# State scaling and diagonal copies moved from VectorE to ScalarE, with loads and selections re-ordered in the first four chunks

## The chip, the cores and the metric

The kernel runs on one core of one Trainium2 chip. The metric is the device time of one execution in microseconds (us). Each engine of the core has its own queue of instructions and works through it in order: TensorE (PE for its matmuls, PEld for its weight loads), VectorE (DVE), ScalarE (ACT), GpSimd (POOL) and SyncE (SP), which here only issues transfers. An instruction that waits for a semaphore holds up everything behind it on the same engine.

## What is computed

A recurrence over time (an RWKV-like attention with a decay) for 4 sequences, 8 heads, 768 steps and head size 48; its output, as 3072 tokens of 384 features, goes through three matrices, their maximum, and a fourth matrix. In short:

```python
for t in range(768):                       # r, k, v, w: (4, 8, 768, 48)
    cur = einsum('bhd,bhe->bhde', u * k[t], v[t])
    y[:, :, t] = einsum('bhd,bhde->bhe', r[t], state + cur)
    state = w[t][..., None] * state + einsum('bhd,bhe->bhde', k[t], v[t])
x = y.transpose(0, 2, 1, 3).reshape(3072, 384)
out = maximum(maximum(x @ w1, x @ w2), x @ w3) @ w_out      # 384 -> 768 -> 384
```

The four matrices arrive in 64-bit floats, the rest in 32-bit.

## The kernel before

Time is cut into chunks of 128 steps, 6 to a sequence, 24 in all (k = 0 to 23). Four chunks make a half of 512 tokens for the second part ("MLP"), of which there are six. The first half is worked with plain 32-bit matmuls.

The order of work is written out by hand. `FRONT` is a string of steps for the first four chunks and the start of the first half; each step is a letter with a chunk number, and each engine meets its own instructions in the string's order. The letters that matter here:

- `b`, `f` the two decay scans of a chunk (L360 and L374, DVE; `b` also copies the chunk's decay to `dec`, L362, ACT); `s` the reciprocal between them; `r` scales k and r (L385, L386, DVE); `d` multiplies r by k for the diagonal (L399, DVE, needs the chunk's second load); `D` sums that on PE (L411).
- `e` copies the diagonal's sums out of PSUM to `cs` (L419), lets POOL select them into the matrix `a` (L427), and issues the load of the next chunk's v (L229, SP). The buffer of chunk 4's v is chunk 1's, so its load waits for chunk 1's last values on PE.
- `X` scores (L449, PE), `M` takes them into `a` (L458, DVE), `T` transposes k (L469, PE) with a copy to `kn` (L471, ACT), `R` reads the state (L482, PE), `U` forms the new state (L492, L496, PE), `S` scales it by the decay into `sstar` (L507), `V` and `Z` make the values (L527, PE), `E` copies them to x (L545, ACT) and, after chunks 2 and 3, issues small transfers within x (L554), three by SP and three by ACT.
- `c` squares the scans for an overflow test (L391, ACT). `n` loads a chunk (L241, SP, two parts). `w` loads one weight tile (L287, SP). `i` converts one (L303, ACT; a later step does L312 and L314 on DVE). `W` runs filler matmuls (L573). `m` and `p` run a group of the MLP, which starts on the x of three chunks (L147), adds the fourth (L155), and goes on with whole groups (L167); the maximum of a group's three results starts with a copy `h_hi` (L130, ACT), which also frees one of three PSUM banks, and goes on with L133 (DVE).

After `FRONT`, `START` and two loops run the rest in the same manner.

Of the kernel before, what the change touches and what calls it, by code (L numbers as in the profile page):

```python
# [34 lines left out]
ALU = mybir.AluOpType  # L35
AF = mybir.ActivationFunctionType
# [4 lines left out]
B, H, S, D = 4, 8, 768, 48  # L41
DM, FF = 384, 768
NP = 4
# [10 lines left out]
CPH = HT // C  # L54
# [12 lines left out]

FRONT = ("b0 s0 f0 d0 W2 D0 W3 r0 X0 T0 W3 c0 e0 b1 s1 d1 D1 U0 f1 W4 R0 e1 M0 V0 Z0 E0 S0 n3 r1 "  # L70
# [3 lines left out]
TURN = "b1 d1 w | f1 w | D1 r1 c1 | e1 M0 w | "  # L74
ORD = "w R0 V0 U0 X1 Z0 E0 b2 d2 | f2 n3 w | D2 S0 r2 c2 | e2 M1 w | T1 w | |"

# [18 lines left out]
def kernel(ctx: ExitStack, tc, tin, nat, u_flat, u_pair, v_t, w_all, out, ytr):  # L95
    nc = tc.nc
# [99 lines left out]
    with ExitStack() as fast:  # L196
# [23 lines left out]
        def load_nat(k):  # L220
            b, c = divmod(k, NCH)
            if k in natt:
                return
            vt = v_p.tile([128, DM], F32, name="v")
            kr = None
            if k >= CS:
                kr = nat_p.tile([128, 2, DM], F32, name="kr")
                nc.sync.dma_start(out=kr[:, :, :], in_=nat[b, c, :, 1:3, :])
            nc.sync.dma_start(out=vt[:, :], in_=nat[b, c, :, 0, :])  # L229
            natt[k] = (vt, kr)  # L230
# [39 lines left out]
        sstar = [cst.tile([128, NP, 64], F32, name=f"sstar{i}") for i in range(2)]  # L270
        dec = [cst.tile([128, LINE], F32, name=f"dec{i}")[:, 0:NP] for i in range(2)]
# [83 lines left out]
        prep = {k: {} for k in range(NK)}  # L355
# [59 lines left out]
        def prep_diag2(k):  # L415
            ahead("D", k)
            cs = small.tile([128, LINE], F32, name="cs")[:, 0:H]
            if k < CS:
                nc.vector.tensor_copy(out=cs[:, :], in_=prep[k]["ps"][:, 0:H])  # L419
            else:  # L420
                nc.vector.tensor_reduce(out=cs[:, :].rearrange("p (a b) -> p b a", a=2),  # L421
                                        in_=natt[k][1][:, 0, :].rearrange("p (b a d) -> p b a d", a=2, d=D),
                                        axis=AX.X, op=ALU.add)
            a = a_p.tile([128, 4, 3, HC], F32, name="a")
            for lo in (0, HC):
                rows = slice(lo, lo + HC)
                nc.gpsimd.affine_select(out=a[rows, :, 0:2, :], pattern=[[0, 4], [0, 2], [1, HC]],  # L427
                                        in_=cs[rows, :].rearrange("p (a b) -> p a b", b=2).unsqueeze(3).broadcast_to([HC, 4, 2, HC]),
                                        compare_op=ALU.is_equal, fill=0.0, base=0, channel_multiplier=-1)
            prep[k]["a"] = a  # L430
            if k + 1 < NK:
                load_nat(k + 1)
# [28 lines left out]
        def goes_on(k):  # L461
            return k % NCH < NCH - 1
# [36 lines left out]
        def state(k):  # L499

            if goes_on(k):
                new = prep[k]["pu"][0:112, 0:NP * D].rearrange("p (a b) -> p a b", a=NP)
                if k % NCH > 0 and k >= CPH:
                    cur = scur[0:112, :].rearrange("p (a b) -> p a b", a=NP)
                    nc.vector.tensor_tensor(out=cur, in0=new, in1=sstar[k % 2][0:112, :, 0:D], op=ALU.add)
                    new = cur
                nc.vector.tensor_tensor(out=sstar[(k + 1) % 2][0:112, :, 0:D], in0=new,  # L507
                                        in1=dec[(k + 1) % 2][0:112, :].unsqueeze(2).broadcast_to([112, NP, D]), op=ALU.mult)

        def after(later, sooner):  # L510

# [27 lines left out]
        def result(k):  # L539
# [11 lines left out]
            for lo in (0, 64) if cols else ():  # L551
                for j in range(KT):
                    eng = nc.scalar if lo and half < PLAIN else nc.sync
                    eng.dma_start(out=x[lo + 48:lo + 64, j, cols], in_=x[lo + 16 * j:lo + 16 * j + 16, KT, cols])  # L554

        steps = dict(X=scores, M=take, T=transposes, R=from_state, U=to_state, S=state, V=values, Z=values2, E=result, n=load,
                     b=prep_scan_b, s=prep_start, f=prep_scan_f, r=prep_rk, c=prep_check, d=prep_diag1,
                     D=prep_diag_sum, e=prep_diag2)
        ready = {("n", k) for k in range(3)}

        def ahead(step, k):

            if k < NK and (step, k) not in ready:
                ready.add((step, k))
                steps[step](k)
# [107 lines left out]
        def take_x(early=False):  # L673
            h = len(xs)
            there = ("E", CPH * (h + 1) - 2) in ready if early else units >= min(UPH * (h + 1) + XD, UPC * NK)
            if h < NH and there and groups >= GPH * h - 2 * CPH:
                xs[h] = x_parts(h)
# [39 lines left out]
        simple = dict(p=part, a=unit, c=weights, i=begin, w=load_w, m=group, f=fix, x=lambda: take_x(True))  # L717
        for step in FRONT.split():
            if step in simple:
# [14 lines left out]
    with tc.If(verdict[0] != 0, label="general"), ExitStack() as slow:  # L734
        pool = lambda name, bufs, **kw: slow.enter_context(tc.tile_pool(name=name, bufs=bufs, **kw))
        c1 = pool("c1", 1)
# [7 lines left out]
        with tc.For_i(0, B) as b:  # L744
            for pr in range(NP):
# [8 lines left out]
                for hh in range(2):  # L754
                    rows = slice(64 * hh, 64 * hh + 48)
                    for t, o in ((wt, pr * WS + 1), (rt, WC + pr * C), (kt, WC + NP * C + pr * C)):
                        for c in range(NCH):
                            for lo in (0, HC):
                                at = o + (HC - lo if t is kt and pr % 2 == 0 else lo)
                                nc.sync.dma_start(out=t[rows, c * C + lo:c * C + lo + HC],  # L760
                                                  in_=tin[ds(b, 1), c, rows, at:at + HC].rearrange("a p n -> (a p) n"))
                    nc.sync.dma_start(out=uc[rows, :], in_=u_pair[pr, hh])
                nc.vector.tensor_scalar(out=uk[0:112, :], in0=kt[0:112, :], scalar1=uc[0:112, :], scalar2=None, op0=ALU.mult)
                for j in range(KT):
                    with tc.For_i(0, 16) as i:
# [5 lines left out]
                        for hh in range(2):  # L771
                            nc.sync.dma_start(
                                out=vb[64 * hh:64 * hh + 48, :],
                                in_=v_t[ds(b, 1), 2 * pr + hh, ds(i + 16 * j, 1), :].rearrange("a e t -> (a e) t").broadcast_to([48, S]))
# [22 lines left out]
        for i in range(NW if w_all.dtype != F32 else 0):  # L797
# [5 lines left out]
            low, scale = raw[:, 0:2 * PC:2], sc[:, :].bitcast(F32)  # L803
# [16 lines left out]
        with tc.For_i(0, NH) as half:  # L820
            x = xs_p.tile([128, KT, HT], F32, name="x")
# [73 lines left out]
```

## Time and profile before

| | |
|---|---|
| runs, us | 413.6, 413.74, 414.51 (median 413.74) |
| profiled execution | 413.68 us, its span 412.0 us |
| PE busy | 400.9 us, 97% of the span |
| DVE, ACT, POOL busy | 279.4, 151.3, 80.6 us |
| granted TensorE clock | 1.00 throughout |
| instructions | 9165 |

Times in rows count from the start of the span. The execution's own time is 1.7 us longer than its span. PE is busy almost without a break from 34.4 us to the end; the first 34 us, where the first four chunks run one after another, have DVE busy for 9.14 to 9.86 us of every 10 us from 10 us on.

### The profile page before, as it was taken

To read this page: it belongs to the slowest core of one execution; us is meant where nothing else is said; L and a number is where in the kernel's file an instruction comes from. 1 tells how busy PE (TensorE), PEld (TensorE's weight loads), DVE (VectorE), ACT (ScalarE), POOL (GpSimd) and SP (SyncE) were. 2 spreads that over 40 slices of the span, in tenths; PEclk is the share of its full clock that TensorE was granted. 3 is DMA by queue.
4 is the path that set the end of the run, shared out by engine and by line. 5 is a ranking of instruction groups with operands and counts; after the bars stand their busy time and mean duration, and the time that the engine had idled before them with its cause. 6 is when DMAs were issued, how large, how long until landed. Compare 5 with 4: busy or idle time off the path is not lost.

```text
span 412.0 us, 9165 instructions
## 1 busy us (share of the span) xinstructions
PE 400.9 (97%) x3729; PEld 315.6 (77%) x3729; DVE 279.4 (68%) x511; ACT 151.3 (37%) x318; POOL 80.6 (20%) x96
## 2 busy tenths in 40 slices
PE   6989999999999999999999999999999999999994
PEld 2656454556688889988889988889988888988894
DVE  6989999989869969848777658678666622233320
ACT  1344434233535532525433644433622321311211
POOL 2410032233222211213122212223123200000000
PEclk9999999999999999999999999999999999999999
DMA  8594994641550330595563686751550000300001
GB/s 210 157 324 143 335 312 140 208 139 40 152 176 23 105 111 17 139 286 163 176 184 113 158 267 212 228 154 43 180 168 2 0 2 2 97 1 0 2 15 66
DMA packets 24126, 54.09 MB, mean 131 GB/s; under 512 B 3312, under 2 KB 9776, under 8 KB 24080
## 3 DMA queue, kind: packets, MB, share of 16 engines
q1 hardware_dynamic: 20160, 43.43, 34.2%
q10 hardware_dynamic: 3920, 10.03, 8.1%
q8 instruction: 30, 0.49, 0.5%
q14 instruction: 16, 0.13, 0.1%
HBM read 47.55 MB, written 4.72 MB: 127 GB/s over the span
## 4 chain that ended last, share of the span: by engine, by line
PE 94%; DMA 1%; ACT 1%; issue 1%; SPq 1%; POOL 0%; POOLq 0%; ACTq 0%
PE psm L167 56%; PE psm L187 16%; PE gram L449 5%; PE y L527 5%; PE tu L492 3%; PE y L482 3%; PE psm L573 2%; PE tu L469 2%; DMA out_dram<-m 1%; PE psm L411 1%; PE psm L147 1%; SPq L554 1%; DMA x<-x 0%; PE psm L155 0%; PE tu L496 0%
## 5 line engine op out<-in xcount | busy, mean ns | idle before, releaser
L167 PE MATMUL psm<-x_hi,w 128*128 128x512 f32 x540 | 172.8, 394 | 0.2 <-ACT m L191 0.2
L167 PEld LDWEIGHTS psm<-x_hi,w 128*128 128x128 f32 x540 | 101.4, 188 | 22.0 <-ACT m L191 0.8
L167 PE MATMUL psm<-x_lo,w 128*128 128x512 f32 x270 | 105.3, 390 | 0.0
L133 DVE TENSOR_TENSOR m<-psm,m 128x512 f32<-128x512 f32 x60 | 41.1, 685 | 58.9 <-PE psm L167 44.5
L187 PE MATMUL psm<-w,h_hi 128*128 128x384 f32 x288 | 78.2, 364 | 0.0
L427 POOL TENSOR_SCALAR_AFFINE_SELECT a<-cs 64x512 f32<-64x512 f32 x48 | 37.1, 774 | 143.4 <-DVE cs L421 92.6
L167 PEld LDWEIGHTS psm<-x_lo,w 128*128 128x128 f32 x270 | 50.8, 188 | 9.8
L187 PEld LDWEIGHTS psm<-w,h_hi 128*128 128x128 f32 x288 | 51.8, 188 | 6.5 <-DVE w L314 0.4
L167 PE MATMUL psm<-x,w 128*128 128x512 f32 x96 | 42.6, 597 | 0.0
L545 ACT COPY x<-y 112x512 f32<-112x512 f32 x24 | 14.1, 586 | 75.2 <-PE y L527 74.7
L402 POOL TENSOR_TENSOR kr<-kr 128x384 f32<-128x384 f32 x18 | 21.1, 1172 | 99.8 <-PE y L527 88.5
L187 PE MATMUL psm<-w,h_lo 128*128 128x384 f32 x120 | 40.3, 336 | 0.0
L391 ACT ACTIVATE gf<-gf 112x1034 f32<-112x1034 f32 x24 | 25.7, 1070 | 35.6 <-DVE tin L386 35.2
L110 ACT CAST h_hi<-m 128x512 fp32r<-128x512 f32 x30 | 18.7, 622 | 53.7 <-DVE m L133 53.7
L374 DVE TENSOR_TENSOR_SCAN gf<-tin,d_fwd 112x517 f32<-112x517 f32 x24 | 36.1, 1502 | 0.7
L167 PEld LDWEIGHTS psm<-x,w 128*128 128x128 f32 x96 | 17.8, 190 | 20.4 <-issue 19.1
L360 DVE TENSOR_TENSOR_SCAN gf<-tin,d_bwd 112x517 f32<-112x517 f32 x24 | 29.9, 1246 | 4.8 <-DMA tin<-in_tin_dram 4.7
L111 DVE TENSOR_TENSOR h_lo<-m,h_hi 128x512 fp32r<-128x512 f32 x30 | 20.6, 688 | 16.7 <-ACT h_hi L110 16.7
L527 PE MATMUL y<-a,v 64*48 64x64 f32 (+3 forms) x768 | 25.7, 246 | 0.6 <-POOLq L534 0.2
L458 DVE COPY_PREDICATED a<-mask,gram 128x384 f32<-128x384 int32 x48 | 25.3, 581 | 0.5 <-PE gram L449 0.5
L527 PEld LDWEIGHTS y<-a,v 64*64 64x64 f32 (+1 forms) x768 | 21.6, 126 | 4.7 <-issue 3.1
L130 ACT COPY m<-psm 128x512 f32<-128x512 f32 x30 | 17.5, 582 | 16.4 <-PE psm L167 9.8
(72 smaller groups left out, 424.9 us busy)
## 6 DMA issues: line engine op xcount, KB each, us to landing
tin<-in_tin_dram SPq DMA_DIRECT2D x23, 448.0 KB, 5.1
w<-in_w_all_dram SPq DMA_DIRECT2D x24, 384.0 KB, 7.2
cv<-in_w_all_dram ACTq DMA_DIRECT2D x24, 384.0 KB, 3.6
kr<-in_nat_dram SPq DMA_DIRECT2D x18, 384.0 KB, 5.8
tin<-in_tin_dram SPq DMA_DIRECT2D x23, 231.0 KB, 3.5
v<-in_nat_dram SPq DMA_DIRECT2D x24, 192.0 KB, 5.5
out_dram<-m SPq DMA_DIRECT2D x24, 192.0 KB, 2.6
x<-x SPq DMA_DIRECT2D x30, 32.0 KB, 2.0
```

The source lines that it names most:

```text
L111: rest = lambda: nc.vector.tensor_tensor(out=lo, in0=src, in1=hi.bitcast(F32), op=ALU.subtract)
L133: nc.vector.tensor_tensor(out=m[:, :], in0=ps[:, :], in1=m[:, :], op=ALU.max)
L167: nc.tensor.matmul(ps[:, :], lhsT=wt[f * 3 + wi][:, ct * 128:(ct + 1) * 128], rhs=xt[:, ct, :], start=(n == 0), stop=(n == KT * len(terms) ...
L187: nc.tensor.matmul(pss[tt][:, 0:DM], lhsT=ht[f][:, tok], rhs=wt[FT * 3 + f][:, :], start=(f == 0 and i == 0), stop=(f == FT - 1 and i == l ...
L360: nc.vector.tensor_tensor_scan(out=gf[0:112, 0, ::-1], data0=t[0:112, 0:WC][:, ::-1], data1=d_bwd[0:112, ::-1], initial=0.0, op0=ALU.mult, ...
L374: nc.vector.tensor_tensor_scan(out=gf[0:112, 1, :], data0=tbuf[k % NB][0:112, 0:WC], data1=d_fwd[0:112, :], initial=0.0, op0=ALU.mult, op1 ...
L391: nc.scalar.activation(out=flat, in_=flat, func=AF.Square, accum_out=acc[0:112, k:k + 1])
L402: nc.gpsimd.tensor_tensor(out=n[:, 0, :], in0=n[:, 0, :], in1=n[:, 1, :], op=ALU.mult)
L427: nc.gpsimd.affine_select(out=a[rows, :, 0:2, :], pattern=[[0, 4], [0, 2], [1, HC]], in_=cs[rows, :].rearrange("p (a b) -> p a b", b=2).un ...
L449: nc.tensor.matmul(to, lhsT=p["kp"][q:q + 48, pr, lo:lo + HC], rhs=p["rp"][q:q + 48, pr, HC * late:C], start=(hh, lo) not in begun, stop=T ...
L458: nc.vector.copy_predicated(out=p["a"][:, 2 * hh:2 * hh + 2, :, :].rearrange("p a b c -> p a (b c)"), mask=mask_b(2), data=p["gs"][hh].rea ...
L527: mm = nc.tensor.matmul(p["y"][64 * half:64 * half + m, hh, j, HC * late:C], lhsT=natt[k][0][lo:lo + HC, h * D:h * D + m], rhs=a[:, j, :] ...
```

## The change

`e` copies the sums by ACT for chunks 0 to 5, where DVE did it. `S` scales the state of chunks 0 to 3 by four ACT instructions, one per pair of heads, where one DVE instruction did it. In `FRONT`, `e` of chunks 0, 2 and 3 stands ahead of the transposes (with it goes the load of the next chunk's v), `S` of chunks 0 to 2 stands directly behind `U` or one step later, the loads of chunks 4 and 5 and of the weights change places, and the third conversion `i` stands behind chunk 2's copy to x.

```diff
-FRONT = ("b0 s0 f0 d0 W2 D0 W3 r0 X0 T0 W3 c0 e0 b1 s1 d1 D1 U0 f1 W4 R0 e1 M0 V0 Z0 E0 S0 n3 r1 "
-         "W2 X1 d2 D2 T1 c1 b2 s2 e2 R1 U1 M1 V1 Z1 E1 f2 S1 n4 w w w r2 "
-         "W4 X2 d3 D3 T2 c2 b3 s3 e3 w w R2 U2 n5 i i i M2 V2 Z2 E2 f3 S2 r3 "
-         "W3 X3 d4 T3 R3 M3 x V3 Z3 E3 w w U3 p p w w c n6 w m D4 b4 s4 c c3 S3 m w f4 c e4 m r4 c X4 T4 R4 c4 w w")
+FRONT = ("b0 s0 f0 d0 W2 D0 W3 r0 X0 e0 T0 W3 c0 b1 s1 d1 D1 U0 f1 W4 R0 e1 S0 M0 V0 Z0 E0 n3 r1 "
+         "W2 X1 d2 D2 e2 T1 c1 b2 s2 R1 U1 S1 M1 V1 Z1 E1 f2 r2 "
+         "W4 X2 d3 D3 e3 w w w n4 w T2 c2 b3 s3 R2 U2 S2 i i M2 V2 Z2 E2 i n5 f3 r3 "
+         "W3 X3 d4 T3 R3 M3 x V3 Z3 E3 w w w U3 p p w c n6 w m D4 b4 s4 c c3 S3 m w f4 c e4 m r4 c X4 T4 R4 c4 w w")
...
-                nc.vector.tensor_copy(out=cs[:, :], in_=prep[k]["ps"][:, 0:H])
+                nc.scalar.copy(out=cs[:, :], in_=prep[k]["ps"][:, 0:H])
...
-                nc.vector.tensor_tensor(out=sstar[(k + 1) % 2][0:112, :, 0:D], in0=new,
-                                        in1=dec[(k + 1) % 2][0:112, :].unsqueeze(2).broadcast_to([112, NP, D]), op=ALU.mult)
+                for pr in range(NP) if k < CPH else ():
+                    nc.scalar.activation(out=sstar[(k + 1) % 2][0:112, pr, 0:D], in_=new[:, pr, :], func=AF.Identity,
+                                         scale=dec[(k + 1) % 2][0:112, pr:pr + 1])
+                if k >= CPH:
+                    nc.vector.tensor_tensor(out=sstar[(k + 1) % 2][0:112, :, 0:D], in0=new,
+                                            in1=dec[(k + 1) % 2][0:112, :].unsqueeze(2).broadcast_to([112, NP, D]), op=ALU.mult)
```

Lines from 508 on lie four further down in the changed kernel (L554 becomes L558). PE's instructions stand in the same order before and after.

SP's queue before, from the load of chunk 3's v on (`v` is L229; `tin_115` is chunk 4's buffer and `tin_116` chunk 5's; `w` are weight tiles):

```order
L229 DMA v<-in_nat_dram 128x384
L241 DMA tin_115<-in_tin_dram 112x528
L241 DMA tin_115<-in_tin_dram 112x1024
L287 DMA w<-in_w_all_dram 128x384 x3
L229 DMA v<-in_nat_dram 128x384
L287 DMA w<-in_w_all_dram 128x384 x2
L241 DMA tin_116<-in_tin_dram 112x528
L241 DMA tin_116<-in_tin_dram 112x1024
L554 DMA x<-x 16x384 x3
L554 DMA x<-x 16x128 x3
L287 DMA w<-in_w_all_dram 128x384 x4
```

SP's queue now, the same stretch:

```order
L229 DMA v<-in_nat_dram 128x384 x2
L287 DMA w<-in_w_all_dram 128x384 x3
L241 DMA tin_115<-in_tin_dram 112x528
L241 DMA tin_115<-in_tin_dram 112x1024
L287 DMA w<-in_w_all_dram 128x384
L558 DMA x<-x 16x384 x3
L241 DMA tin_116<-in_tin_dram 112x528
L241 DMA tin_116<-in_tin_dram 112x1024
L558 DMA x<-x 16x128 x3
L287 DMA w<-in_w_all_dram 128x384 x4
```

Chunk 4's v and three weight tiles stand ahead of chunk 4's load, four weight tiles instead of five stand ahead of the transfers within x, and the fifth tile stands behind the second set of them.

ACT's queue before, from the second set of transfers within x on (`cv` is the conversion of the next weight tile, here the fourth to the seventh):

```order
L554 DMA x<-x 16x128 x3
L303 ACTIVATE cv<-w,minus_two 128x384
L362 COPY dec_137<-gf 112x4
L303 ACTIVATE cv<-w,minus_two 128x384
L391 ACTIVATE gf,acc<-gf 112x1034
L130 COPY h_hi<-psm 128x512
L303 ACTIVATE cv<-w,minus_two 128x384 x2
```

ACT's queue now, the same stretch:

```order
L558 DMA x<-x 16x128 x3
L303 ACTIVATE cv<-w,minus_two 128x384
L362 COPY dec_137<-gf 112x4
L303 ACTIVATE cv<-w,minus_two 128x384
L391 ACTIVATE gf,acc<-gf 112x1034
L508 ACTIVATE sstar_135<-tu,dec_137 112x48 x4
L130 COPY h_hi<-psm 128x512
L303 ACTIVATE cv<-w,minus_two 128x384
L419 COPY cs<-psm 128x8
L303 ACTIVATE cv<-w,minus_two 128x384
```

The conversions of the fourth and fifth tile stand where they stood; four scalings of chunk 3's state now stand ahead of the copy `h_hi`, and the copy of chunk 4's sums stands between the sixth and seventh tile's conversions.

## Rows read from the trace of the kernel before

**Rows 1.** The page, busy time by engine, and instruction queue (packets, MB, share):

```profile
PE 400.9 (97%) x3729; PEld 315.6 (77%) x3729; DVE 279.4 (68%) x511; ACT 151.3 (37%) x318; POOL 80.6 (20%) x96
...
q8 instruction: 30, 0.49, 0.5%
```

**Rows 2.** Who waited for whom, PE, whole span (total us, times, longest):

```profile
PE tu L492 <- issue: 1.4, 1, 1.4
PE psm L167 <- ACT m L191: 0.2, 1, 0.2
```

**Rows 3.** Chain of waits, 20 to 48 us (start, us, what):

```profile
25.74 1.35 issue
...
34.53 3.87 PE psm L147 x12
...
40.49 2.58 PE psm L167 x6
```

**Rows 4.** Timeline of DVE (start, us, instruction, idle time before and its releaser):

```profile
9.35 0.17 DVE L419 COPY cs<-psm 128x8 f32<-128x8 f32 x1 [0.27 <-PE psm L411]
...
20.60 0.32 DVE L507 TENSOR_TENSOR sstar<-tu,dec 112x192 f32<-112x192 f32 x1
20.84 0.90 DVE L385 TENSOR_TENSOR tin<-tin,gf 112x256 f32<-112x256 f32 x2
...
28.00 0.36 DVE L507 TENSOR_TENSOR sstar<-tu,dec 112x192 f32<-112x192 f32 x1 [0.79 <-ACT cv L303]
...
29.54 0.75 DVE L399 TENSOR_TENSOR kr<-tin 112x256 f32<-112x256 f32 x2
30.77 1.05 DVE L458 COPY_PREDICATED a<-mask,gram 128x384 f32<-128x384 int32 x2 [0.47 <-PE gram L449]
```

**Rows 5.** Timeline of PE, up to 46 us:

```profile
21.34 1.04 PE L573 MATMUL psm<-warm 128*128 128x512 bf16 x4
...
29.73 0.90 PE L449 MATMUL gram<-tin 48*64 48x128 f32 x32
...
40.33 2.74 PE L167 MATMUL psm<-x,w 128*128 128x512 f32 x6
```

**Rows 6.** Timeline of SP's issues, 18 to 38 us:

```profile
18.80 0.79 SPq L241 DMA_DIRECT2D tin<-in_tin_dram  x2
...
21.47 0.33 SPq L229 DMA_DIRECT2D v<-in_nat_dram  x1
...
35.63 2.00 SPq L287 DMA_DIRECT2D w<-in_w_all_dram  x4
```

**Rows 7.** DMA issues at 15.99, 21.47, 35.63, then 35.63 with 36.26: us to landing

```profile
v<-in_nat_dram SPq DMA_DIRECT2D x1, 192.0 KB, 2.4
...
v<-in_nat_dram SPq DMA_DIRECT2D x1, 192.0 KB, 6.4
...
w<-in_w_all_dram SPq DMA_DIRECT2D x1, 384.0 KB, 3.4
...
w<-in_w_all_dram SPq DMA_DIRECT2D x2, 384.0 KB, 4.3
```

**Rows 8.** Busy time by stretch, 26 to 30 us (last: clock, DMA share, GB/s):

```profile
26.00:30.00 4.00, 2.79 (x47) 1.76 (x51) 3.21 (x7) 2.44 (x6) 0.13 (x1) 1.00 1.04 351
```

**Rows 9.** Timeline of ACT, 25 to 40 us:

```profile
25.97 0.19 ACT L362 COPY dec<-gf 112x4 f32<-112x4 f32 x1
26.06 1.93 ACT L303 ACTIVATE cv<-w,minus_two 128x384 f32<-128x384 uint32 x3
...
36.61 0.65 ACT L303 ACTIVATE cv<-w,minus_two 128x384 f32<-128x384 uint32 x1
37.16 1.05 ACT L391 ACTIVATE gf<-gf 112x1034 f32<-112x1034 f32 x1
38.12 0.19 ACT L391 ACTIVATION_READ_ACCUMULATOR gf<-gf 112x1 f32 x1
39.10 0.58 ACT L130 COPY h_hi<-psm 128x512 f32<-128x512 f32 x1 [0.80 <-PE psm L155]
```

## The prediction, on record before the changed kernel ran

> **What bounds the kernel now.** I read the page first: PE is busy for 97% of the span [rows 1]. So the second question is where PE waits at all, and the list of its waits has next to nothing: one gap of 1.4 us in the front, called "issue", and 0.2 us much later [rows 2]. The chain of waits says the same in order of time: from 34.5 us on it runs along PE, L147, L155 and L167 without a break [rows 3]. What follows has a fixed length as long as PE never waits. The time therefore changes by two things only: how early PE enters L147, and whether it is held up afterwards. The timelines of the front tell the rest. There DVE sets the pace, and its last long wait is the one for U of chunk 2, behind PE's gap [rows 3, 4].
>
> **What DVE is spared.** The first copy of sums takes 0.17 us, after a wait of 0.27 us for PE; without it the next scan starts about 0.4 us sooner [rows 4]. The later copies are worth some 0.06 us each, since they overlap with their neighbours. The state scaling of chunk 1 takes 0.24 us of DVE's queue (20.60 to 20.84), that of chunk 2 as much again and a wait of 0.79 us that would only grow were DVE earlier [rows 4]. By the end of chunk 1 DVE is 1.0 us ahead (0.4, two scalings of 0.25, two copies). PE is less ahead, because its values and fillers of that chunk stay: I take 0.4 us at the end of chunk 1's second values (before: 21.34, where the fillers begin [rows 5]), with 0 and 0.8 as ends. The selections ahead of the transposes cost nothing: POOL has 20% of its time in use [rows 1], and its order is unchanged. What the added copies cost ACT in chunks 0 to 3 is covered too: ACT waits for PE or DVE before most of what it does there.
>
> **PE's gap.** At 25.74 PE stops for 1.35 us [rows 3] and nothing it needs is missing. PE's 7458 instructions stand against 30 packets of 16 KB on the instruction queue [rows 1], so some 249 fit a packet, and I read the gap as a packet that came late through transfers that were queued from 18.80 on [rows 6]. In the changed order nothing large is issued between chunk 3's v (15.99) and the end of chunk 1's values, so this packet should come in time and the gap go. Then chunk 2's values end near 27.0, about 2 us sooner, and with them DVE's wait for U.
>
> **What is late next.** Chunk 4's load is. On SP it used to be issued at 18.80; now it stands behind the load of chunk 4's v, which waits for chunk 1's second values as it did before (issued 21.47, just after 21.34 [rows 5, 6]), and behind three weight tiles. So it starts after about 21.07 (21.47 less 0.4). Its landing: before, the same six loads (231 and 448 KB of chunk 4, three tiles of 384 KB, 192 KB of v, 2023 KB in all) were issued from 18.80 on, and the last landed at 21.47 + 6.4 = 27.87 [rows 6, 7], 9.07 us after the first issue. The same bytes from 21.07 on end at 30.1, and now chunk 4's second part is the last. That is the nearest row, and I take it. The other end: a lone v lands in 2.4 us [rows 7], of which its 197,000 bytes take 0.56 us at 351 GB/s [rows 8], so 1.84 us are fixed; with 2.07 MB at that rate (5.9 us) the six end 7.7 us after 21.07, at 28.8. A later end, 30.6, is had with no gain on PE and 0.1 us more.
>
> DVE's multiply of chunk 4 (L399) needs that load, and chunk 3's take (L458) stands behind it on DVE. Before, L399 started at 29.54 and could have released the take 0.65 us later, but the take waited for scores until 30.77 [rows 4]. Now L399 starts at about 30.15 and the take at 30.8. **Nothing is left of the gain**: chunk 3's values, U and L147 stand where they stood, within -2.0 (the take can't precede the scores, 29.73 before [rows 5] plus 0.9 and then about 2 us sooner) and +0.5 us. The weights for L147 are converted by DVE right behind the take and move with it. The transfers within x after chunk 2 are issued by ACT and SP around 28 to 31 instead of 29.73 on, behind two conversions instead of three, and have landed well before L147. Chunk 5's load, now behind them, is wanted only at chunk 5, 12 us later, and costs nothing.
>
> **What is added: the fifth weight tile.** It used to be issued before chunk 5's load. Now it stands on SP behind the second transfers within x, in the place that the sixth tile had: issued at 35.63, landing 3.4 us later, at 39.03 [rows 6, 7]. Its conversion stands on ACT ahead of the overflow square, of the four new scalings and of `h_hi`, and was done at 36.61 before [rows 9]. So ACT now waits until 39.06. From there by rows 9: conversion to square 0.55 (36.61 to 37.16), square to its accumulator 0.96 (37.16 to 38.12), 0.09 to the next (as 25.97 to 26.06), then four scalings. For those no row exists; the copies of decay are the nearest, small ones of 0.19 us that follow each other by 0.09 us, so four take 0.36 to 0.8 us; I take 0.5, near the lower end since they queue without waits. `h_hi` then starts at 39.06 + 0.55 + 0.96 + 0.09 + 0.5 = 41.16 and ends 0.58 later, at 41.74, where before it started at 39.10 [rows 9]. PE's next group (L167, third tile) writes the bank that `h_hi` empties; it started at 40.33 [rows 5] and now starts at 41.8: **a new wait of 1.45 us**. Queued behind `h_hi` are L133 on DVE, and behind that chunk 4's scaling of r and scores; these move by about as much and add nothing of their own. The ends: with the tile landing in 3.0 us (as the fixed 1.84 and 1.12 for its bytes) and four scalings at 0.36, 0.9; with 4.3 us, what the median of two tiles shows [rows 7], and 0.8, 2.65.
>
> [...]
>
> **Sum.** Profiled execution 413.68 us (0.06 under the median of the runs); entry into L147 unchanged (0.0), new wait +1.45: **415.1 us**.
>
> **Rivals.**
> 1. *Chunk 4's load lands early.* At 28.8 the take starts at 29.5 instead of 30.77: 413.68 - 1.3 + 1.45 = 413.8. For it: six loads at the rate of rows 8 would do so. Against: the same six took 9.07 us before. It decides at about 29.4: landing before that, the kernel is not slower by more than 0.2%. This is the other side.
> 2. *Early load and early tile.* If the take reaches the scores (-2.0) and the new wait is only 0.9 to 1.1, 412.7. For it: PE could be up to 0.8 us ahead when v is issued. Against: it needs both ends at once.
> 3. *PE's next instruction packet comes late.* The backlog now lies 2.3 us later, across the packet after the one that was late; a second gap like the first adds 1.35: 416.5. For it: rows 3 show one such gap under such a backlog. Against: nothing after it showed one, though transfers were queued. [...]
>
> **Chances.** Differences under 0.2% (0.8 us) can hardly be told from no change here. Forecast 0.55 (its own range 414.3 to 416.2, of which 0.05 lies under 414.5), rival 1 0.20, rival 2 0.12, rival 3 0.13. So slower by over 0.2% 0.50 + 0.13 = 0.63, within 0.05 + 0.20 = 0.25, faster 0.12. The range leaves out most of rival 2 and the upper half of rival 3: 412.9 to 416.5.
>
> **What would show it.** Right: no gap in PE before chunk 2's U; L399 of chunk 4 waiting for `tin` until about 30; L147 within 0.5 us of 34.5; ACT waiting for `w` until about 39; L167 of the third tile waiting for `h_hi`, starting near 41.8, and no PE wait after that. Wrong: L399 without a wait, or L147 before 33 (rival 1, 2); another gap called "issue" (rival 3); `h_hi` before 40, which would mean that the fifth tile came earlier than I read from SP's order.

## The result: 1.3% slower, and outside the range

The changed kernel takes **419.28 us** (median; 418.43 to 419.49), the kernel before 413.85 us on the same chip: ratio **1.0131, 95% interval 1.0108 to 1.0154**, 5.4 us more. The direction was forecast, the size was not: 415.1 us, with 416.5 as the upper end. The profiled execution took 418.43 us, the shortest of the four, with a span of 416.6 us (before: 413.68 and 412.0). Executions of one kernel differ with the clock: of 25 of the kernel before, the ten with a mean granted clock of 0.998 or more took 413.05 us on the mean and the three below 0.990 416.17, and the profiled one had 1.000, while all of the kernel after had 0.986 to 0.990.

In the changed file the lines from the state scaling on stand four further down: the values L527 are now L531, the fillers L573 are L577. First PE's list of waits in the kernel after (engine, line, releaser: total us, times, longest), which had two rows of note before [rows 2]:

```profile
PE y L531 <- DVE a L458: 4.1, 1, 4.1
...
PE psm L167 <- ACT h_hi L130: 1.2, 1, 1.2
```

PE's gap of 1.35 us is gone, as forecast. The wait for `h_hi` is there, 1.2 us long, as forecast (a wait of 3.2 us at the start, which is left out here, is the same in either kernel). But there is a wait of 4.1 us for chunk 3's take, which the prediction had put at nothing. The timeline of PE shows both and what lies between (start, us, instruction, idle time before it and its releaser):

```profile
24.28 0.67 PE L492 MATMUL tu<-v,kn 128*64 128x48 f32 x16
...
28.66 0.66 PE L482 MATMUL y<-tin,sstar 48*64 48x128 f32 x16
33.39 2.43 PE L531 MATMUL y<-a,v 64*64 64x128 f32 x32 [4.07 <-DVE a L458]
...
37.55 4.47 PE L147 MATMUL psm<-x,w 128*128 128x384 f32 x12
...
45.30 2.84 PE L167 MATMUL psm<-x,w 128*128 128x512 f32 x6 [1.20 <-ACT h_hi L130]
```

The same places in the kernel before:

```profile
31.59 1.55 PE L527 MATMUL y<-a,v 64*48 64x128 f32 x32
...
34.36 4.04 PE L147 MATMUL psm<-x,w 128*128 128x384 f32 x12
```

Three steps make up the loss. Chunk 3's values start **1.80 us** later (33.39 against 31.59), although the scores ahead of them were ready sooner. From there to L147 PE needs 4.16 us instead of 2.77, **1.39 us** more, without waiting: each instruction is slower. From L147 to the third tile (before at 40.33 [rows 5]) it takes 7.75 instead of 5.97, **1.78 us** more: the wait for `h_hi` and the slower L147. Together 4.97 us. What follows has nearly the same length in both: span less start of the third tile is 371.3 us after and 371.7 before. So these traces hold 4.6 us of the 5.4 that the medians show.

Why the second step is slower is seen in the busy time by stretch (the last three columns: granted TensorE clock, DMA share, GB/s):

```profile
24.00:29.00 5.00, 4.85 (x113) 3.37 (x106) 3.17 (x6) 3.83 (x11) 0.78 (x2) 1.00 0.93 279
29.00:33.00 4.00, 0.32 (x12) 0.08 (x4) 0.92 (x3) 1.05 (x2) 0.00 (x0) 0.82 0.69 166
33.00:38.00 5.00, 4.53 (x51) 3.76 (x52) 4.90 (x9) 0.59 (x1) 0.00 (x0) 0.50 0.50 143
```

Behind the wait the granted clock is 0.50 until about 38 us. Values that take 1.55 us take 2.43 there.

The wait's cause stands on DVE and on SP (start, us, instruction):

```profile
32.08 0.76 DVE L399 TENSOR_TENSOR kr<-tin 112x256 f32<-112x256 f32 x2 [4.92 <-DMA tin<-in_tin_dram]
32.76 1.04 DVE L458 COPY_PREDICATED a<-mask,gram 128x384 f32<-128x384 int32 x2
```

```profile
15.41 5.76 SPq L229 DMA_DIRECT2D v<-in_nat_dram  x2
21.23 2.23 SPq L287 DMA_DIRECT2D w<-in_w_all_dram  x3
23.55 0.84 SPq L241 DMA_DIRECT2D tin<-in_tin_dram  x2
24.44 0.43 SPq L287 DMA_DIRECT2D w<-in_w_all_dram  x1
28.04 2.89 SPq L558 DMA_DIRECT2D x<-x  x3
...
36.50 1.78 SPq L558 DMA_DIRECT2D x<-x  x3
38.33 2.01 SPq L287 DMA_DIRECT2D w<-in_w_all_dram  x4
```

Chunk 4's `v` was issued at 20.83 (the first row holds two issues and ends with this one, at 21.17; one takes 0.35), three weight tiles follow, and chunk 4's load only at 23.55. L399 has to wait for it until 32.08, and the take stands behind L399 on DVE: 32.76 against 30.77 [rows 4].

### The profile page after: what moved, and what is told of

It reads as the page before. It is cut to its first block, busy times and chain, and to the rows that moved or that the text cites. A ratio compares the mean times of both kernels' runs of the same rounds, so it can differ in the third digit from the quotient of the medians.

```text
span 416.6 us, 9182 instructions
## 1 busy us (share of the span) xinstructions
PE 402.2 (97%) x3729; PEld 316.9 (76%) x3729; DVE 277.9 (67%) x501; ACT 154.8 (37%) x340; POOL 80.7 (19%) x96
## 4 chain that ended last, share of the span: by engine, by line
PE 92%; DMA 3%; ACT 2%; issue 1%; DVE 1%; SPq 1%; POOL 0%; POOLq 0%; ACTq 0%
PE psm L167 54%; PE psm L187 16%; PE y L531 5%; PE gram L449 4%; PE tu L492 3%; PE y L482 3%; PE psm L577 2%; PE tu L469 2%; DMA x<-x 2%; PE psm L147 1%; DMA out_dram<-m 1%; PE psm L411 1%; SPq L558 1%; PE tu L496 0%; PE psm L155 0%
## 5 line engine op out<-in xcount | busy, mean ns | idle before, releaser
L167 PE MATMUL psm<-x_hi,w 128*128 128x512 f32 x540 | 172.9, 394 | 0.2 <-ACT m L191 0.2
L167 PEld LDWEIGHTS psm<-x_hi,w 128*128 128x128 f32 x540 | 101.4, 188 | 22.0 <-ACT m L191 0.8
L167 PE MATMUL psm<-x_lo,w 128*128 128x512 f32 x270 | 105.3, 390 | 0.0
L167 PEld LDWEIGHTS psm<-x_lo,w 128*128 128x128 f32 x270 | 50.8, 188 | 9.8
L167 PE MATMUL psm<-x,w 128*128 128x512 f32 x96 | 42.7, 598 | 1.2 <-ACT h_hi L130 1.2
L167 PEld LDWEIGHTS psm<-x,w 128*128 128x128 f32 x96 | 17.8, 190 | 21.8 <-issue 19.0
L531 PE MATMUL y<-a,v 64*48 64x64 f32 (+3 forms) x768 | 26.5, 251 | 4.6 <-DVE a L458 4.1
L531 PEld LDWEIGHTS y<-a,v 64*64 64x64 f32 (+1 forms) x768 | 22.3, 129 | 9.0 <-DVE a L458 4.7
```

What stands on the lines that cost most here:

```text
L167: nc.tensor.matmul(ps[:, :], lhsT=wt[f * 3 + wi][:, ct * 128:(ct + 1) * 128], rhs=xt[:, ct, :], start=(n == 0), stop=(n == KT * len(terms) ...
L531: mm = nc.tensor.matmul(p["y"][64 * half:64 * half + m, hh, j, HC * late:C], lhsT=natt[k][0][lo:lo + HC, h * D:h * D + m], rhs=a[:, j, :] ...
```

## The experiments

All ran beside the kernel before. Its median was 413.8 to 413.9 us beside the runs e and f, and 414.4 beside the runs g, which were taken on another chip; so it is the ratios that compare across groups, and not the times. The times first, and from each profile the two starts that decide:

| kernel | us | ratio, 95% interval | L147 starts | third tile (L167) | span |
|---|---|---|---|---|---|
| before | 413.85 | 1 | 34.36 | 40.33 | 412.0 |
| after | 419.28 | 1.0131 (1.0108 to 1.0154) | 37.55 | 45.30 | 416.6 |
| e1_load4_first | 415.47 | 1.0030 (1.0003 to 1.0056) | 33.17 | 41.74 | 413.0 |
| e2_tile5_first | 417.59 | 1.0087 (1.0055 to 1.0119) | 38.16 | 44.95 | 415.9 |
| e3_both_first | 412.39 | 0.9973 (0.9946 to 1.0000) | 32.31 | 38.52 | 410.0 |
| e4_engines_only | 418.77 | 1.0115 (1.0075 to 1.0156) | 40.22 | 47.99 | 419.0 |
| f1_fillers | 416.48 | 1.0067 (1.0037 to 1.0097) | 36.49 | 42.76 | 414.5 |
| f2_loads_alone | 417.00 | 1.0087 (1.0055 to 1.0118) | 38.09 | 45.67 | 417.3 |
| f3_behind_v_only | 416.56 | 1.0055 (1.0029 to 1.0081) | 36.71 | 44.14 | 415.8 |
| f4_both_kn_first | 412.56 | 0.9979 (0.9950 to 1.0009) | 32.00 | 38.77 | 410.5 |
| g1_before_loads | 413.59 | 0.9980 (0.9956 to 1.0004) | 34.73 | 42.24 | 412.9 |
| g2_kn_on_dve | 410.43 | 0.9915 (0.9889 to 0.9941) | 31.69 | 37.68 | 408.3 |
| g3_dve_good_loads | 412.70 | 0.9966 (0.9946 to 0.9986) | 33.49 | 39.70 | 411.1 |

Span less third tile lies between 370.6 and 371.7 us in every row. So the front decides nearly alone, as the prediction read from the chain of waits [rows 3], and the third tile's start is the number to follow. The edits are all in the third and fourth line of the order, and only the steps that differ are shown.

**Is it the two late loads?** One, the other, or both go ahead:

```diff
 e1: -D3 e3 w w w n4 w T2
     +D3 n4 e3 w w w w T2
 e2: -D3 e3 w w w n4 w T2 ... E3 w w w U3
     +D3 e3 w w w n4 w w T2 ... E3 w w U3
 e3: -D3 e3 w w w n4 w T2 ... E3 w w w U3
     +D3 n4 e3 w w w w w T2 ... E3 w w U3
```

> The changed kernel with chunk 4's load back ahead of chunk 4's v and the tiles, all else as changed. Theory A (the place of the loads on SP costs the time: chunk 4's multiply waits 4.9 us for its load, PE's clock falls to 0.50 in the gap, and the fifth tile holds up the copy h_hi): no wait of L399, granted clock 1.00 throughout, L147 near 32.3 instead of 37.6, the wait for h_hi of about 1.2 us stays; time 412.9 us. Rival B (the scalings and copies on ScalarE cost the time, whatever the loads): little moves, 417 us or more.

> The changed kernel with the fifth weight tile back among the loads ahead of the transfers within x, all else as changed. Theory A: the wait of L167 for h_hi (1.2 us) goes, the wait for chunk 4's load and the low clock stay; 418.0 us. Rival B: no change, 419.3 us. Rival C (a tile more in the backlog delays the transfers within x by as much as is gained): 419.3 us.

> The changed kernel with chunk 4's load ahead and the fifth tile back: ScalarE's work and the selections as changed, only these loads as before. Theory A: no wait of PE after chunk 2, clock 1.00, L147 near 32.3; 411.7 us, faster than the kernel before. Rival B: 417 us or more.

With both, 6.9 us of the changed kernel's time go, and it is level with the kernel before or a little faster (412.39 us, close to the 411.7 expected). With chunk 4's load alone it is 415.47, short of the 412.9 expected; the reasons stand in PE's rows of e1_load4_first (first that for the third chunk's state sums):

```profile
31.98 0.67 PE L492 MATMUL tu<-v,kn 128*64 128x48 f32 x16 [1.18 <-ACT kn L471]
...
33.17 5.54 PE L147 MATMUL psm<-x,w 128*128 128x384 f32 x12
...
41.74 2.84 PE L167 MATMUL psm<-x,w 128*128 128x512 f32 x6 [0.93 <-ACT h_hi L130]
```

The take is no longer late (L147 starts at 33.17), but a next wait comes to light, for ACT's copy `kn`; the granted clock falls again (0.68 on the mean from 31 to 36 us) and L147 takes 5.54 us instead of 4.04; and the fifth tile still holds `h_hi`, for 0.93 us. In e2_tile5_first that last wait is gone, the wait for the take remains (4.53 us), and so does the half clock (0.50 from 33 to 38 us). Only the two together undo the loss.

**Engines alone, loads alone.** The order and loads of before with the code on ScalarE (e4), and the code of before with the loads of after (f2):

```diff
 e4: the order and loads of before; L419 and L508 on nc.scalar as in the change
 f2: the code of before;
     -E1 f2 S1 n4 w w w r2 W4 X2 d3 D3 T2 c2 b3 s3 e3 w w R2 U2 n5 i i i M2 V2 Z2 E2 f3 S2 r3
     +E1 f2 S1 r2 W4 X2 d3 D3 e3 w w w n4 w T2 c2 b3 s3 R2 U2 i i M2 V2 Z2 E2 i n5 f3 S2 r3
     -E3 w w U3 p p w w c
     +E3 w w w U3 p p w c
```

(With the loads, f2 also takes over the place of the third conversion `i`, behind chunk 2's copy to `x`.)

> The order of steps of the kernel before, with the scalings and the copies of sums on ScalarE. Theory A: the moves to ScalarE cost nothing, PE's gap of 1.35 us stays or shrinks; 413.0 us, within 0.7. Rival B: the moves cost the most of the 5.4 us; 417 us or more.

> The kernel before, with VectorE's copies and scalings as they were, but with the loads in the changed order: chunk 4's load behind chunk 4's v and three weight tiles, the fifth tile behind the second transfers within x. Theory: the loss is made by the loads alone. L399 of chunk 4 waits for its load until about 32, PE waits some 3 to 4 us for the take, the clock falls to 0.50, and the fifth tile holds h_hi, this time without the four scalings (0.7 us less): about 418.5. Rival: without the earlier engines nothing is lost, since PE itself comes only at 30: 414 to 415.

f2 says that the loads need no engine's help to do harm: 417.0 us (expected 418.5), and L399 and the values wait as after:

```profile
32.64 0.76 DVE L399 TENSOR_TENSOR kr<-tin 112x256 f32<-112x256 f32 x2 [3.39 <-DMA tin<-in_tin_dram]
```

```profile
33.95 2.42 PE L527 MATMUL y<-a,v 64*64 64x128 f32 x32 [2.62 <-DVE a L458]
```

The fifth tile did not hold PE this time, against what was expected: `h_hi` itself waited for PE, until 44.45.

e4 was expected at 413.0 and took 418.77: my theory fell there. The loss has two parts in its profiled execution, which at 420.74 us is one of the two longest of six. The first is early. With the old order ACT copies chunk 0's sums behind its overflow square, at 11.96 instead of 9.35 [rows 4]; POOL selects them only then, the first take waits for POOL (1.31 us), and PE for the take (1.05) (timeline of PE, then busy time by stretch, with clock, DMA share, GB/s last):

```profile
14.25 1.74 PE L531 MATMUL y<-a,v 64*64 64x128 f32 x32 [1.05 <-DVE a L458]
```

```profile
17.00:20.00 3.00, 3.00 (x52) 2.59 (x48) 2.93 (x6) 0.50 (x4) 0.00 (x0) 0.50 0.24 66
```

From 20 to 30 us the clock is 0.66 on the mean, and the fillers behind chunk 1's values start at 24.66 instead of 21.34 [rows 5], 3.3 us late. The other executions took 417.42 to 420.83 us, and no trace shows whether their clock fell there too. The second part comes in chunk 2: the four scalings stand on ACT behind three conversions, the copy to `x` and the issue of three transfers (timelines of ACT and PE in e4_engines_only):

```profile
30.26 1.73 ACT L303 ACTIVATE cv<-w,minus_two 128x384 f32<-128x384 uint32 x3
31.89 0.56 ACT L549 COPY x<-y 112x512 f32<-112x512 f32 x1
32.49 2.32 ACTq L558 DMA_DIRECT2D x<-x  x3
34.86 0.87 ACT L508 ACTIVATE sstar<-tu,dec 112x48 f32<-112x48 f32 x4 [2.40 <-issue]
```

```profile
35.79 0.60 PE L469 MATMUL tu<-ident,tin 112*128 112x112 f32 x4 [2.65 <-ACT sstar L508]
```

So the move between engines can't be judged without the move in the order that comes with it: in e4 the scalings came only at 34.86, behind 4.60 us of conversions, copy and issues on ACT from 30.26 on. The step stood behind ACT's long ones there; in the changed order it stands ahead of them.

**The load's place: behind `v`, or behind three tiles?** Chunk 4's load stays behind chunk 4's `v`, but goes ahead of the tiles:

```diff
-D3 e3 w w w n4 w T2
+D3 e3 n4 w w w w T2
```

> The kernel after with chunk 4's load behind chunk 4's v but ahead of all weight tiles (the fifth tile stays late). Theory: the bytes of the three tiles ahead make the load late, not v's wait: chunk 4's load issued near 21.3 lands by 28, L399 does not wait, chunk 3's take comes at about 28.3, and the time is that of e1_load4_first, 415.5. Rival: the later start costs as much by itself, L399 waits until 30 or later, PE waits over 2 us and the time is 417 or more.

The theory's first half holds: L399 doesn't wait, so it was the three tiles ahead that made the load late (DVE in f3_behind_v_only):

```profile
27.27 0.76 DVE L399 TENSOR_TENSOR kr<-tin 112x256 f32<-112x256 f32 x2
```

Its second half does not: 416.56 us. Now the weight tiles are late, and ACT waits for them ahead of its copy to `x`, which PE needs (ACT, then PE):

```profile
28.19 0.65 ACT L303 ACTIVATE cv<-w,minus_two 128x384 f32<-128x384 uint32 x1 [1.70 <-DMA w<-in_w_all_dram]
30.45 0.64 ACT L303 ACTIVATE cv<-w,minus_two 128x384 f32<-128x384 uint32 x1 [1.60 <-DMA w<-in_w_all_dram]
30.98 0.57 ACT L549 COPY x<-y 112x512 f32<-112x512 f32 x1
```

```profile
31.61 0.66 PE L482 MATMUL y<-tin,sstar 48*64 48x128 f32 x16 [2.81 <-ACT x L549]
```

Both orders tried behind `v` have a wait for a load: 4.92 us of L399 for chunk 4's in after, 1.70 and 1.60 us of ACT for the tiles in f3. Ahead of `v`, as in e1 and e3, chunk 4's load is not waited for (L399 at 27.18 and 27.01, without a wait); in e3 SP issues nothing else between 18.91 and 20.75 us.

**Is the half clock a cost of its own?** The kernel of e2 with 14 fillers on PE where it waits for the take; nothing else differs:

```diff
-T3 R3 M3 x V3
+T3 R3 W14 M3 x V3
```

> The kernel after with the fifth tile's load ahead (as in e2_tile5_first) and, in addition, 14 filler multiplications of 128x512 on PE behind chunk 3's state products (L482), where PE waited 4.53 us for the take and then ran at a granted clock of 0.50. Theory: the half clock follows from PE's idleness, so with the wait filled the clock stays at 1.00; from the take to L147 PE needs 2.5 us instead of 4.16 and L147 3.9 instead of 4.7, together 2.5 us less: about 415.1 against 417.6. The wait itself is not shortened: V3 (L531) still starts near 34. Rival: the clock has another cause (the transfers, the conversions), it falls all the same, and the time stays at 417.6; if the fillers run past the take it gets worse.

Busy time by stretch, f1_fillers, then e2_tile5_first:

```profile
28.00:33.00 5.00, 4.56 (x50) 2.27 (x42) 0.49 (x2) 1.13 (x3) 0.00 (x0) 1.00 0.97 267
33.00:38.00 5.00, 3.98 (x55) 2.93 (x56) 4.90 (x10) 0.59 (x1) 0.00 (x0) 1.00 0.59 158
```

```profile
28.00:33.00 5.00, 1.47 (x39) 1.02 (x28) 0.30 (x1) 1.17 (x3) 0.00 (x0) 1.00 0.98 295
33.00:38.00 5.00, 3.91 (x50) 3.26 (x51) 4.90 (x11) 0.59 (x1) 0.00 (x0) 0.50 0.54 163
```

With PE kept busy the clock stays at 1.00; the values start no sooner (33.82 against 34.00), but the third tile starts at 42.76 instead of 44.95, 2.19 us earlier. Of that the span keeps 1.4 us and the median 1.1 us (417.59 to 416.48, where 2.5 less was expected; the two ratios' intervals overlap). The mean granted clock of the executions carries it too: 0.994 to 1.000 in all ten of f1, 0.984 to 0.991 in all eight of e2. The clock follows from PE's idleness here, and not from transfers or conversions, which are nearly the same in the rows above.

**Was PE's old gap really a matter of the loads?** All engines' programs of after, word for word, with SP's loads where they were before:

```diff
-E1 f2 r2 W4 X2 d3 D3 e3 w w w n4 w T2 ... i i M2 V2 Z2 E2 i n5 ... E3 w w w U3
+E1 f2 n4 w w w r2 W4 X2 d3 D3 e3 w w T2 ... i i M2 V2 Z2 E2 i n5 ... E3 w w U3
```

> The kernel after, word for word the same on PE, DVE, ACT and POOL, with only SP's loads back in the places that they had before (chunk 4's load and three weight tiles ahead of chunk 4's v, two tiles behind it). Theory: the loads alone cost the 5.4 us; with them back L399 and h_hi wait for no load. PE's gap of 1.35 us in chunk 2 comes back, because the instruction packet stands behind the same transfers as before, so most of what VectorE is spared stays unseen: L147 starts near 34, 413 to 413.9, the same as before within 0.2%. Rival: the gap does not come back (it had to do with something else), L147 starts near 32.3 and the time is that of e3_both_first, 412.4.

```profile
24.31 0.61 PE L492 MATMUL tu<-v,kn 128*64 128x48 f32 x13
26.33 0.29 PE L492 MATMUL tu<-v,kn 128*64 128x48 f32 x3 [1.41 <-issue]
```

The gap is back, 1.41 us, in the same group of instructions where the kernel after has none, and SP's loads are all that differs. The instruction queue's packet moves at 24 to 25 us before and at 23 to 24 here, against 21 to 22 in after, and in e3_both_first, where only chunk 4's load stands ahead of `v` and the tiles behind it. That the gap is this packet's coming late fits all four traces, but no run moved the packet alone. Behind this gap the clock fell too (0.50 between 28 and 30 us), which it had not done in the profiled execution of the kernel before behind nearly the same gap. The engine move gains next to nothing with the old loads: ratio 0.998, an interval that holds 1. It isn't the gap alone that hides it: further on PE waits another 1.28 us, until 40.49, for the transfers within `x`.

**A faster version, and what the engine move is worth.** From e3_both_first, three ways on. f4 moves a conversion behind `kn`; g2 copies chunk 3's `kn` on DVE behind the take, takes two fillers away, puts chunk 2's copy to `x` ahead of the second conversion and chunk 5's load behind the transfers within `x` (chunk 3's copy to `x` still stands behind all three conversions, as in e3, although the text expected of g2 says otherwise); g3 has e3's loads, and its place of the third conversion, with the code and order of before:

```diff
 f4: -E2 i n5 f3 r3 W3 X3 d4 T3 R3 M3 x V3
     +E2 n5 f3 r3 W3 X3 d4 T3 i R3 M3 x V3
 g2: -S2 i i M2 V2 Z2 E2 i n5 f3 r3 W3 X3 ... V3 Z3 E3 w w U3
     +S2 i M2 V2 Z2 E2 i f3 r3 W1 X3 ... V3 Z3 i E3 n5 w w U3
     -nc.scalar.copy(out=kn, in_=pt)          # in transposes(k)
     +if k == CPH - 1: p["pt"] = pt           # and at the end of take(k):
     +    nc.vector.tensor_copy(out=p["kn"], in_=p["pt"])
 g3: -E1 f2 S1 n4 w w w r2 W4 X2 d3 D3 T2 c2 b3 s3 e3 w w R2 U2 n5 i i i M2 V2 Z2 E2 f3 S2 r3
     +E1 f2 S1 r2 W4 X2 d3 D3 n4 e3 w w w w w T2 c2 b3 s3 R2 U2 i i M2 V2 Z2 E2 i n5 f3 S2 r3
     -E3 w w U3 p p w w c
     +E3 w w U3 p p w c
```

> The kernel e3_both_first (chunk 4's load and five tiles ahead) with the third tile's conversion on ACT moved behind chunk 3's copy of transposes (kn). Theory: PE's wait of 0.68 us for kn came from that conversion, which itself waited for the tile until 30.18; the wait goes to 0.1 or less, L147 starts at 31.7 instead of 32.31: 411.7 against 412.4. Rival: kn stands behind the three transfers within x that ACT issues until 30.13 and the gain is under 0.2, or L147 then waits for its third tile, which is converted 0.5 us later: 412.2 to 412.6.

> A version meant to be faster than both. Like e3_both_first, with chunk 3's copy of transposes (kn) on VectorE behind the take, two fillers fewer ahead of chunk 3's scores (DVE waited 0.49 us for those), chunk 2's and chunk 3's copies to x each ahead of one conversion more on ACT, and chunk 5's load behind the transfers within x. Theory: PE's wait for kn (0.68) goes, the take starts 0.45 earlier, and the first transfers within x land near 31.5 instead of 32.22: L147 starts at 31.6 instead of 32.31, about 411.7. Rival: the transfers within x or the weight tiles, which land until 31.1, set L147's entry in any case: 412.2 to 412.8.

> The loads of e3_both_first (chunk 4's load first, five tiles behind chunk 4's v) with VectorE's copies and scalings and their order as before. What the engine move is worth by itself, where no load is late. Theory: PE's gap is gone here too, and DVE is about 1 us later than in e3_both_first at chunk 3's take (29.3 against 28.25), so L147 starts near 33.2: 413.2. Rival: the moves are worth nothing behind kn's wait and the transfers within x, L147 starts within 0.3 us of 32.3: 412.4.

f4 gained nothing (412.56). The tile whose landing I had named had come in time; what held ACT until 30.13 was its own issue of three transfers. `kn` moved by 0.33 us, and the second transfers within `x` went out later and held PE for 0.5 us instead. g2 is **the fastest, 410.43 us, 0.85% under the kernel before**, and PE goes from the values to L147 without a wait:

```profile
29.21 1.54 PE L536 MATMUL y<-a,v 64*48 64x128 f32 x32
30.68 0.67 PE L497 MATMUL tu<-v,kn 128*64 128x48 f32 x16
...
31.69 4.05 PE L147 MATMUL psm<-x,w 128*128 128x384 f32 x12
```

The take itself is no earlier than in e3 (28.38 against 28.25); what I expected of the fillers did not come, since the scores then waited for DVE (0.29 us). Which of the other edits gained most was not taken apart. Part of the 0.85% goes with the clock: g2's six executions all have a mean of 0.997 or more, and the seven of the kernel before beside them with 0.998 or more took 412.78 us on the mean, 2.3 above g2. g3 shows the engine move where no load is late: the third tile starts at 39.70 against 38.52 in e3, 1.2 us of difference in the trace. The times don't show it: against the kernel before on its own chip g3 has a ratio of 0.9966 and e3 of 0.9973. So what the engine move is worth in time stays open. L147 came at 33.49, near the 33.2 expected.

## Why the prediction was wrong

**What DVE is spared: right.** PE's fillers behind chunk 1's values start at 20.70 instead of 21.34 [rows 5], 0.64 us earlier (forecast 0.4, between 0 and 0.8). e3 and g3, which differ in these moves and their order alone, are 1.2 us apart at L147 in one trace each; their ratios don't tell them apart.

**PE's gap: right.** It went (the run of 16 at 24.28 above), chunk 2's values ended 2.4 us sooner (forecast 2), and g1 brought it back by the loads alone; that a late packet makes it fits the traces, as said, and isn't shown by itself. Two traces here have such a gap, 1.35 us (before) and 1.41 us (g1). The rival of a second gap didn't come about.

**What is late next: the right load, the wrong size, and this is the step that failed.** The prediction let six loads take 9.07 us from the first issue, as before, and had the last land at 30.1, at 30.6 at the latest. It landed shortly ahead of 32.08, 11.2 us after the first issue at 20.83. The start is not what differs: in either kernel nothing was under way when the first of the six was issued (18.80 before, 20.83 after). The last of the six was issued 3.2 us after the first, where it was 2.7, and landed 8.0 us after its own issue, where it was 6.4. The rows from the first issue on, before and then after (last columns: DMA share, GB/s):

```profile
18.00:20.00 2.00, 1.91 (x38) 1.41 (x36) 1.93 (x7) 1.52 (x4) 1.23 (x2) 1.00 0.15 20
20.00:22.00 2.00, 1.88 (x38) 1.15 (x36) 2.00 (x5) 0.68 (x3) 1.13 (x1) 1.00 0.95 323
22.00:24.00 2.00, 1.98 (x52) 1.52 (x51) 2.00 (x4) 0.06 (x1) 0.00 (x0) 1.00 0.99 326
24.00:26.00 2.00, 1.65 (x34) 1.14 (x32) 1.93 (x7) 1.51 (x4) 1.19 (x2) 1.00 0.99 356
```

```profile
20.00:22.00 2.00, 1.88 (x42) 1.07 (x38) 2.00 (x7) 1.16 (x5) 0.00 (x0) 1.00 0.10 21
22.00:24.00 2.00, 2.00 (x65) 1.78 (x56) 1.93 (x5) 0.47 (x2) 0.54 (x1) 1.00 0.84 273
24.00:26.00 2.00, 1.91 (x46) 1.23 (x35) 2.00 (x4) 1.82 (x7) 0.78 (x2) 1.00 0.81 223
26.00:28.00 2.00, 1.94 (x51) 1.34 (x51) 1.17 (x3) 2.00 (x6) 0.00 (x0) 1.00 1.00 339
28.00:30.00 2.00, 1.32 (x32) 0.87 (x24) 0.00 (x0) 0.02 (x1) 0.00 (x0) 1.00 1.02 258
```

Over the six busy microseconds that follow the first row, the engines moved 335 GB/s on the mean before and 278 after. Three things stand beside this. SP's issue of the three tiles took 2.23 us, where it took 1.37 before. The DMA engines stood still for a sixth of the time from 22 to 26 us. And from 28 us on the transfers within `x` shared the engines with the load, at 258 GB/s; in the kernel before they came only after the last landing, and the prediction, which saw them come at 28 to 31 us, charged the load nothing for them. The fourth tile, issued right behind the load, weighs less: with a fifth behind it too (f1_fillers, which has e2's loads) L399 started 11.58 us after the first issue (32.51 against 20.93) instead of 11.25. None of these had a term, none was taken away by itself, and why the same six loads moved more slowly in this order stays open. The price of the miss: the take at 32.76 instead of the forecast 30.8, and since the scores had become early, a wait of 4.1 us on PE. The upper bound was the worse mistake: 30.6 moved the start of the loads, but held their duration fixed. With the measured landing the prediction's own sum would be about 417.1 us (415.1 and the 1.96 by which the take was late), already outside the range; the clock comes on top of it.

**The clock: no term at all.** In the trace of before the clock is 1.00 from 20 to 32 us, behind the gap too, so that nothing in that trace asked for one. But I forecast that PE, early by 2 us, would wait for a late take, and never asked what state it would come out of the wait in. In after this costs 1.39 us up to L147 and 0.43 in it; with the wait filled (f1 against e2) the stretch up to L147 is 1.49 us shorter, and L147 takes 4.04 us instead of 4.85.

**The fifth tile: right in mechanism and nearly in size, on a base that had moved.** SP's second transfers within `x` stand behind chunk 3's values, so the tile was issued at 38.33 instead of 35.63, 2.70 us later, for the forecast "unchanged". From its landing on (timeline of ACT in after):

```profile
42.33 0.64 ACT L303 ACTIVATE cv<-w,minus_two 128x384 f32<-128x384 uint32 x1 [2.94 <-DMA w<-in_w_all_dram]
42.88 1.05 ACT L391 ACTIVATE gf<-gf 112x1034 f32<-112x1034 f32 x1
...
43.93 0.85 ACT L508 ACTIVATE sstar<-tu,dec 112x48 f32<-112x48 f32 x4
44.66 0.59 ACT L130 COPY h_hi<-psm 128x512 f32<-128x512 f32 x1
```

The tile took 4.0 us (forecast 3.4, up to 4.3), conversion to scalings 1.60 us as in [rows 9], and the four scalings 0.73 us from their start to that of `h_hi` (43.93 to 44.66), where I took 0.5. The spacing of 0.09 us behind the decay copy in [rows 9] was too short a measure: these four come to 0.18 us each. PE's wait became 1.20 us, for a forecast of 1.45, only because PE too was late.

**In sum**, of the 4.97 us at the third tile 1.80 are the take, 1.82 the clock (1.39 and 0.43), and 1.2 the fifth tile; the remaining 0.15 isn't explained. The forecast had 0, nothing, and 1.45. Taking causes away gives a like picture in the medians: the fifth tile 1.7 us (419.28 to 417.59), the clock 1.1 (to 416.48), and from there 4.1 to e3_both_first, where the take isn't late either and the gain on PE and DVE shows. The chance of 0.63 for slower was on the right side, and for a reason that the forecast gave, the fifth tile; the range failed because its upper end went by the same six-load duration as the forecast, and had no clock in it.

## What to carry to other kernels

When a load is put behind a wait, the duration of its group can't be carried over from another order: here the same six loads took 9.07 us in one order and 11.2 in the other, both times from idle DMA engines. Let the upper bound vary the duration and not only the start, and look at what is issued ahead of the load and what shares the engines with it. A wait of some microseconds on PE can be dearer than its length (in after 4.07 us, and 1.39 us more from the values to L147 at a clock of 0.50): look at the granted clock behind it. Where it fell here, fillers gave a part back (f1 against e2: the third tile 2.19 us earlier), while the values started no sooner. And moving small work to another engine in order means moving it ahead of that engine's long work; by itself it can cost more than it spares (e4, 418.77 us). And one trace is one execution: set its granted clock against that of the others before a cause is read from it.

## What the runs showed of the hardware that was not expected

- After an idle stretch of 4.07 us PE ran at a granted clock of 0.50 from 33 to 38 us; with fillers in a stretch of that kind (f1) at 1.00.
- It fell behind PE's waits of 2.62 us (f2: 0.65 on the mean from 33 to 38 us, 0.58 from 38 to 42), 2.65 (e4: 0.50 from 38 to 40), 2.81 (f3: 0.50 from 33 to 38) and 4.53 (e2: 0.50 from 33 to 38) as well. Shorter stretches went either way. Behind 1.05 us (e4) the clock was 0.50 from 17 to 20 us, behind 1.18 us (e1) 0.68 on the mean from 31 to 36, behind 1.41 us (g1) 0.50 from 28 to 30; behind 1.35 us (before), 1.20 us (the second wait of after) and 0.68 us (e3), 1.26 us (f1, behind the fillers) and 1.28 us (g1, the second) it stayed at 1.00. These are single executions, and those of the kernel before have mean clocks from 0.984 to 1.000, so that its gap of 1.35 us may be followed by a fall in others. What decides between them these runs don't show.
- The instruction packet moved two to three microseconds later where chunk 4's load and three tiles had been issued ahead of `v` (at 24 to 25 us in before and 23 to 24 in g1, against 21 to 22 in after and e3); in these two traces (before, g1) PE stopped for 1.35 and 1.41 us.
